# A tenth load for ten DMA engines: 640 columns of w1 on other partitions, and two engines that end in new blocks of instructions

## The chip, the cores and the metric

The kernel runs on one core of a Trainium2 chip. The metric is device microseconds of one execution; the number compared is the median of a few runs. Sixteen DMA engines serve the core, through a queue that SyncE (SP) issues on (q1, hardware) and one that GpSimd (POOL) issues on (q0, software). Instructions arrive by DMA too (q8).

## What is computed

One decode step for two batch rows: attention with grouped heads over the last 4096 positions of a cache, a dense layer with Mish beside it, and a gate that mixes both. All data are float32.

```python
# B=2, D=512, Hq=32, Hkv=8, Dh=128, W=4096, F=1792
x = A_x                                        # [2, 1, 512]
g = sigmoid((x * gate_w).sum(-1, keepdims=True))
q = (x @ wq).reshape(B, 1, Hq, Dh).transpose(0, 2, 1, 3)
k = repeat(k_cache[:, :, Sk - W:, :], 4, axis=1)
v = repeat(v_cache[:, :, Sk - W:, :], 4, axis=1)
p = softmax(einsum("bhqd,bhkd->bhqk", q, k) * Dh ** -0.5)
a = einsum("bhqk,bhkd->bhqd", p, v).transpose(0, 2, 1, 3).reshape(B, 1, Hq * Dh) @ wo
h = x @ w1 + b1                                # Dense -> Mish -> Dense
b = (h * tanh(softplus(h))) @ w2
out = g * a + (1 - g) * b
```

## The kernel before

**Stages.** 91 MB come from HBM once. SyncE issues nearly all loads, each 128 partitions wide, in the order of use: `wq` (8 MB), `small`, then for each of the eight KV heads one load of 8 MB (`kv0` to `kv7`: keys and values of both batch rows), then `w12` (most of w1, and the first rows of wo and w2), the parts of w1 described below, the rest of wo in two loads (5 and 2 MB), and the rest of w2 in three (1024, 512 and 256 KB). Three large buffers (`stream`) rotate, so a load waits until TensorE has finished with the buffer three loads earlier. For each head TensorE computes `scores`, VectorE the maximum, ScalarE the exponential, TensorE turns it (`turned`) and multiplies with the values (`values`). When the last head is done come `hidden` (h = x w1, in `hp`; Mish follows on ScalarE, GpSimd and VectorE), `outputs` (the heads' factors, `ol`), `project` (wo, and the first part of w2, summed in `acc`) and `finish` (the rest of w2, summed in `fin`). A copy and the store end the program. Instructions of each engine run in the order written; `pin` keeps the scheduler from moving one.

**w1 and its moved columns.** w1 has 512 rows, four blocks of 128 (`c` = 0 to 3), and 1792 columns, which `hidden` takes in four groups `j` of 512, 512, 512 and 256. The four groups write to four quarters of `hp`'s partitions. In the last block (c = 3) the 512 columns of group 0 are not part of `w12`. Their 128 rows lie elsewhere: in `ext`, a piece of the buffer of wo, `SLOTS` = 3 rows to a partition, on the partitions that `ROWS_OF` lists (first partition, count, slots). GpSimd clears `ext` with a memset first; the matching values of x stand in `x32[:, 4:7]`, with zeros for all other places. So `hidden` multiplies three slots with `x32` in place of one block. `w12` rows are that much shorter.

**The parts.** Each entry of `ROWS_OF` is one load (`part`). SyncE issues three of them, from five, five and four rows of HBM; GpSimd issues `part2`, eight partitions from two rows of HBM. The number of rows of HBM (`SPLIT`) is the number of DMA engines that share a load. GpSimd issues a tiny load `turn` of seven engines ahead of `part2` and one behind it: 7 + 2 + 7 = 16.

The lines that the prediction's steps touch: the memset of `ext` (L316), `part` (L320), `turn` (L324), the matmuls of `hidden` (L258), `acc` (L348), `fin` (L358), the copy `asum` (L374), and `landed` (L386), where SyncE waits for the last eight loads ahead of the store (L392).

Of the kernel before, what the change touches and what calls it, by code (L numbers as in the profile page):

```python
# [8 lines left out]
F32 = mybir.dt.float32  # L9
# [4 lines left out]
P = 128  # L14
# [12 lines left out]
Q = 32  # L27
RS = Q // B
BH = B * REP
F = 1792  # L30
DC = D // P
FC = F // P
FG = 4
# [1 line left out]
CHUNK = 8192  # L35
HEAD = 2048
SLOTS = 3
APART = ((0, FG),)
WIDTH = sum(n for _, n in APART) * P
ROWS_OF = ((0, 20, 3), (32, 20, 2), (60, 8, 3), (28, 4, 1))  # L40
SPLIT = (5, 5, 2, None)
TURN = 7
GAP = 64
PITCH = 272
W1 = DC * F - WIDTH
# [11 lines left out]
def decode_kernel(ctx: ExitStack, tc: tile.TileContext, res, stored, small, wqh, wqt, kv_in, w12, wo, w2, *rest):  # L57
    *parts, before, behind, out = rest
    nc = tc.nc

    stream = ctx.enter_context(tc.tile_pool(name="stream", bufs=3))
    const = ctx.enter_context(tc.tile_pool(name="const", bufs=1))
# [5 lines left out]
    loads = []  # L68

    def load(name, *parts):  # L70
        t = stream.tile([P, 2 * CHUNK], F32, tag="s", name=name)
        x = 0
        for cols, src in parts:
            loads.append(nc.sync.dma_start(t[:, x : x + cols], src))  # L74
            x += cols
        return t
# [11 lines left out]
                      reason="ScalarE begins behind the first load")  # L88
# [16 lines left out]
    x32 = const.tile([P, DC + SLOTS, Q], F32, name="x32")  # L105
# [51 lines left out]
    pin = tc.keep_in_program_order  # L157

    def scores(kv, t):
        sc = ps_s.tile([P, 512], F32, tag="sc", name=f"sc{kv}")  # L160
        for m in range(BN):
            for j in range(NJ):
                nc.tensor.matmul(sc[Q * j : Q * j + Q, :], qz[:, kv, m * Q : m * Q + Q],  # L163
                                 t[:, (m * NJ + j) * 512 : (m * NJ + j + 1) * 512],
                                 start=(m == 0), stop=(m == BN - 1))
        nc.vector.tensor_reduce(mx[:, kv : kv + 1], sc, axis=AX.X, op=ALU.max, negate=True)  # L166
        p = work.tile([P, 512], F32, tag="p", name=f"p{kv}")
        nc.scalar.activation(p, sc, AF.Exp, bias=mx[:, kv : kv + 1], accum_out=ls[:, kv : kv + 1])  # L168
        return p
# [74 lines left out]
    def hidden(t):  # L244
        hp = ps_s.tile([P, FG * P], F32, tag="sc", name="hp")
        away = dict(APART)
        for c in range(DC + SLOTS):
            for j in range(NJ):
                n = min(FG, FC - j * FG) * P
                if c < DC - 1:  # L250
                    w = t[:, c * F + j * FG * P :]
                elif j in away and c >= DC:
                    w = ext[:, c - DC, P * sum(k for i, k in APART if i < j) :]
                elif j not in away and c == DC - 1:
                    w = t[:, c * F + P * (j * FG - sum(k for i, k in APART if i < j)) :]
                else:
                    continue
                nc.tensor.matmul(hp[Q * j : Q * j + Q, :n], x32[:, c, :], w[:, :n],  # L258
                                 start=(c == 0), stop=(c == (DC + SLOTS if j in away else DC) - 1))
        hs = work.tile([P, FG * P], F32, tag="p", name="hs")  # L260
        nl = (FC - (NJ - 1) * FG) * P
        nc.scalar.copy(hs[:, :nl], hp[:, :nl])
        nc.scalar.copy(hs[: Q * (NJ - 1), nl:], hp[: Q * (NJ - 1), nl:])
        ht = ps_1.tile([P, FG, NJ, Q], F32, tag="pt", name="ht")

        def m(name):
            return const.tile([P, FC, B], F32, name=name)

        h, e, nu, de, ho = (m(x) for x in ("h", "e", "nu", "de", "ho"))
        for k in range(FG):  # L270
            nj = len(range(k, FC, FG))
# [23 lines left out]
    for kv in range(HKV):  # L295
        t = load(f"kv{kv}", (2 * CHUNK, kv_in[kv][:, : 2 * CHUNK]))
        p = scores(kv, t[:, :CHUNK])
# [16 lines left out]
    x = (WO[-1] - WO[0]) * REP * D  # L314
    ext = wo_t[:, x : x + SLOTS * WIDTH].rearrange("p (s w) -> p s w", s=SLOTS)
    nc.gpsimd.memset(ext, 0.0)  # L316

    def part(engine, i):
        p0, n, slots = ROWS_OF[i]
        loads.append(pin(engine.dma_start(ext[p0 : p0 + n, :slots, :].rearrange("p s x -> p (s x)"),  # L320
                                          parts[i][:, : n * slots * WIDTH // parts[i].shape[0]])))

    def turn(name, src):
        pin(nc.gpsimd.dma_start(const.tile([2 * TURN, 2], F32, name=name), src[:, :4]))  # L324

    turn("turn0", before)
    part(nc.gpsimd, 2)
    turn("turn1", behind)
    for i in (0, 1, 3):
        part(nc.sync, i)  # L330
    x = 0
    for cols, src in flat(wo, [f - WO[0] for f in WO], REP * D):
# [2 lines left out]
    x = AHEAD + CUTS[1] * D  # L335
    for cols, src in flat(w2, [f - CUTS[1] for f in CUTS[1:]], D):
        loads.append(nc.sync.dma_start(w12_t[:, x : x + cols], src))
        x += cols
    hidden(w12_t)
    outputs(kf, r)  # L340

    acc = ps_1.tile([P, D], F32, tag="acc", name="acc")
# [25 lines left out]
    for x in range(HQ):  # L368
        w = w12_t[:, W1 + x * D :] if x < first else wo_t[:, (x - first) * D :]
# [1 line left out]
            middle(0, CUTS[1])  # L371
        pin(project(x % REP, oT[:, x, :], w[:, :D], n_of[x % REP]))
    asum = work.tile([P, D], F32, tag="p", name="asum")
    nc.scalar.copy(asum, acc)  # L374

    def output(i):
        for f in range(CUTS[i], CUTS[i + 1]):
# [5 lines left out]
    output(2)  # L383
    output(3)

    landed = nc.sync.nop()  # L386
    for ld in loads[-8:]:
        tc.add_manual_dep(landed.ins, ld.ins.name,
                          mybir.DependencyInfo(mybir.DependencyClass.Sync, mybir.DependencyReason.DATA),
                          reason="SyncE sees the last loads land ahead of the store")  # L390
# [5 lines left out]
                      reason="the store reads the copy")  # L396
# [72 lines left out]
```

## Time and profile before

| | |
|---|---|
| median of 3 runs | 218.88 us (218.82, 218.88, 220.08) |
| the profiled run | 218.95 us |
| its span (first to last instruction) | 217.1 us |
| DMA | 91.38 MB, mean 421 GB/s |
| TensorE busy | 113.3 us (52%) |
| instruction loads (q8) | 6 packets, 0.10 MB |
| GpSimd's queue (q0) | 144 packets, 0.05 MB |

The page of the profile shows busy shares, queues, the chain of work that ended last and the costliest groups of instructions. A group reads: line, engine, operation, tile written <- tiles read. `w` is the tile of `w12`, `wo` holds `ext` as well. The span leaves 218.95 - 217.1 = 1.85 us of the run outside.

### The profile page before, as it was taken

Reading aid. Unit: us, or ns where it says so; the run is one execution under the profiler, and the core shown is the slowest. Engines: PE = TensorE matmul, PEld = TensorE weight load, DVE = VectorE, ACT = ScalarE, POOL = GpSimd, SP = SyncE. Lnnn points to the kernel's source line nnn. Section 1 sums busy time; section 2 is a strip of 40 time slices with the busy share of each in tenths; the row PEclk is TensorE's granted clock in tenths of the full one; section 3 lists DMA queues with packets and bytes.
Section 4 is the critical chain, followed back from the end, with each engine's and each line's share of the span. In section 5 each row is a group of like instructions: output and inputs, shape, how many; then the busy total and the mean of one; then the engine's idle time right before and its main releaser. Section 6 shows DMA issues by size and latency. Waiting matters only on the chain.

```text
span 217.1 us, 1858 instructions
## 1 busy us (share of the span) xinstructions
PE 113.3 (52%) x826; PEld 34.5 (16%) x826; DVE 21.5 (10%) x32; ACT 15.4 (7%) x34; POOL 11.4 (5%) x34
## 2 busy tenths in 40 slices
PE   0000797367055609533770753287066608759995
PEld 0000312112011102101120210012011101213342
DVE  0000000010001320100105010010501001250100
ACT  0200001011002000200010020002002000301001
POOL 8000000000000000000000000000000230100300
PEclk9999999889859975996797699679958957999699
DMA  9798998999989998999999999999999999999894
GB/s 362 338 507 351 546 411 386 399 522 423 399 386 519 426 411 386 495 447 399 399 483 450 399 411 447 483 399 411 450 471 399 423 447 430 430 383 468 377 410 159
DMA packets 2752, 91.38 MB, mean 421 GB/s; under 512 B 566, under 2 KB 646, under 8 KB 954
## 3 DMA queue, kind: packets, MB, share of 16 engines
q1 hardware_dynamic: 2602, 91.24, 97.6%
q8 instruction: 6, 0.10, 0.2%
q0 software_dynamic: 144, 0.05, 0.1%
HBM read 91.24 MB, written 0.04 MB: 421 GB/s over the span
## 4 chain that ended last, share of the span: by engine, by line
DMA 78%; PE 15%; ACT 2%; SPq 2%; DVE 1%; issue 1%; POOL 1%; ACTq 0%
DMA kv<-in_kv 61%; DMA w<-in_w 17%; PE sc L163 8%; PE o L187 5%; ACT p L168 1%; PE fin L358 1%; DVE mx L166 1%; SPq L320 1%; PE pp L175 1%; ACT pT L176 1%; POOL wo L316 1%; SPq L333 0%; SPq L74 0%; SPq L80 0%; DVE res L391 0%
## 5 line engine op out<-in xcount | busy, mean ns | idle before, releaser
L163 PE MATMUL sc<-kv,qz 128*32 128x512 f32 x256 | 43.3, 839 | 54.7 <-DMA kv<-in_kv 54.7
L187 PE MATMUL o<-kv,pT 128*32 128x512 f32 x256 | 29.5, 596 | 5.8 <-ACT pT L176 5.8
L163 PEld LDWEIGHTS sc<-kv,qz 128*32 128x32 f32 x256 | 9.7, 149 | 87.7 <-DMA kv<-in_kv 61.3
L143 PE MATMUL qp<-wq,x 128*32 128x512 f32 x64 | 11.4, 760 | 23.1 <-POOL x L107 23.1
L166 DVE TENSOR_REDUCE mx<-sc 128x1 f32<-128x512 f32 x8 | 5.5, 692 | 112.3 <-PE sc L163 112.3
L168 ACT ACTIVATE p<-sc,mx 128x512 f32<-128x512 f32 x8 | 5.5, 687 | 131.2 <-DVE mx L166 131.2
L175 PE MATMUL pp<-ident,p 128*128 128x128 f32 x32 | 5.2, 286 | 12.1 <-ACT p L168 12.1
L187 PEld LDWEIGHTS o<-kv,pT 128*32 128x32 f32 x256 | 7.3, 109 | 20.9 <-issue 13.2
L316 POOL MEMSET wo<- 128x1536 f32 x1 | 1.4, 1377 | 144.4 <-PE o L187 144.4
L197 DVE TENSOR_REDUCE od<-om 128x256 f32<-128x1024 f32 x4 | 7.6, 1898 | 0.1
L143 PEld LDWEIGHTS qp<-wq,x 128*32 128x32 f32 x64 | 2.4, 134 | 28.7 <-POOL x L107 23.1
L348 PE MATMUL acc<-wo,padded 128*32 128x512 f32 x56 | 6.9, 593 | 0.0
L194 DVE TENSOR_TENSOR om<-o,pick 128x1024 f32<-128x1024 f32 x4 | 4.9, 1225 | 19.3 <-PE o L187 19.3
L175 PEld LDWEIGHTS pp<-ident,p 128*128 128x128 f32 x32 | 3.4, 140 | 18.6 <-ACT p L168 18.6
L176 ACT COPY pT<-pp 128x512 f32<-128x512 f32 x8 | 4.7, 585 | 6.2 <-PE pp L175 6.2
L258 PE MATMUL hp<-w,x 128*32 128x512 f32 (+1 forms) x30 | 3.6, 540 | 2.5 <-DMA w<-in_w 2.5
L348 PE MATMUL acc<-w,padded 128*32 128x512 f32 x22 | 4.3, 896 | 0.4 <-DVE padded L241 0.4
L348 PEld LDWEIGHTS acc<-wo,padded 128*32 128x32 f32 x56 | 2.5, 109 | 3.5 <-issue 2.5
L258 PE MATMUL hp<-wo,x 128*32 128x512 f32 x6 | 2.7, 592 | 0.0
L132 DVE RECIPROCAL g<-g 128x2 f32<-128x2 f32 x1 | 0.2, 165 | 22.4 <-POOL g L131 22.4
L358 PE MATMUL fin<-w,padded 128*32 128x128 f32 x56 | 2.1, 277 | 0.4 <-DMA w<-in_w 0.4
L149 PE MATMUL qt<-ident,qs 128*128 128x128 f32 x8 | 1.3, 286 | 1.4 <-ACT qs L146 1.4
(71 smaller groups left out, 35.8 us busy)
## 6 DMA issues: line engine op xcount, KB each, us to landing
wq<-in_wqt SPq DMA_DIRECT2D x1, 7168.0 KB, 21.5
w<-in_w SPq DMA_DIRECT2D x1, 6144.0 KB, 41.3
wo<-in_wo SPq DMA_DIRECT2D x1, 5120.0 KB, 29.6
wo<-in_wo SPq DMA_DIRECT2D x1, 2048.0 KB, 34.1
wq<-in_wqh SPq DMA_DIRECT2D x1, 1024.0 KB, 4.9
w<-in_w SPq DMA_DIRECT2D x1, 1024.0 KB, 36.0
w<-in_w SPq DMA_DIRECT2D x1, 512.0 KB, 35.4
w<-in_w SPq DMA_DIRECT2D x1, 256.0 KB, 21.1
```

The lines of the kernel that those rows point to most:

```text
L143: nc.tensor.matmul(qp[Q * k : Q * k + Q, :], x32[:, c, :], w[:, c, k, :], start=(c == 0), stop=(c == DC - 1))
L163: nc.tensor.matmul(sc[Q * j : Q * j + Q, :], qz[:, kv, m * Q : m * Q + Q], t[:, (m * NJ + j) * 512 : (m * NJ + j + 1) * 512], start=(m == ...
L166: nc.vector.tensor_reduce(mx[:, kv : kv + 1], sc, axis=AX.X, op=ALU.max, negate=True)
L168: nc.scalar.activation(p, sc, AF.Exp, bias=mx[:, kv : kv + 1], accum_out=ls[:, kv : kv + 1])
L175: pin(nc.tensor.transpose(pp[:, c, :], p[:, c * P : (c + 1) * P], ident))
L176: nc.scalar.copy(pT, pp)
L187: pin(nc.tensor.matmul(o[Q * j : Q * j + Q], pT[:, c, Q * j : Q * j + Q], t[:, (c * NJ + j) * 512 : (c * NJ + j + 1) * 512], start=(c == 0 ...
L194: nc.vector.tensor_tensor(ov, pair[0].rearrange("p k (m d) -> p k m d", m=BN), pick[:, None, :, None].to_broadcast([P, 2, BN, DH]), op=ALU ...
L197: nc.vector.tensor_reduce(od[:, kv - 1 : kv + 1], ov.rearrange("p k m d -> p k d m"), axis=AX.X, op=ALU.add)
L258: nc.tensor.matmul(hp[Q * j : Q * j + Q, :n], x32[:, c, :], w[:, :n], start=(c == 0), stop=(c == (DC + SLOTS if j in away else DC) - 1))
L348: return nc.tensor.matmul(acc[Q * j : Q * j + Q, :], lhsT, rhs, start=(n_col[j] == 1), stop=(n_col[j] == n))
L358: nc.tensor.matmul(fin[Q * j : Q * j + Q, :], lhsT[:, y : y + Q], rhs[:, j * P : (j + 1) * P], start=(done[0] == 0), stop=(done[0] == n_fi ...
```

## The change

Three things change together.

1. 640 columns of w1's last block are moved instead of 512 (`APART`): all of group 0 and the first 128 of group 1. Rows of `w12` get 512 bytes shorter, `ext` gets wider (3 x 640 = 1920 columns instead of 1536), and `hidden` takes group 1 in two pieces: 384 columns from `w12` at c = 3, and 128 columns from `ext` at each of the three slots.
2. The 128 rows lie on other partitions (0 to 19, 32 to 48, 60 to 67 and 84 to 95), and the loads are shared differently: `part0` (20 partitions, 3 slots, five groups), `part1` (five partitions, one slot, five groups), `part2` (three partitions, one slot, three groups) from SyncE, and `part3` (eight partitions, 3 slots, two groups) and `part4` (twelve partitions, 3 slots, three groups) from GpSimd. `turn1` shrinks from seven rows to four: 7 + 2 + 4 + 3 = 16. Five, two and three engines carry parts, ten in all.
3. ScalarE, behind its last copy `asum`, and SyncE, behind a new wait for the last load but one (`early`), jump to the start of a new block of 256 instructions.

```diff
-APART = ((0, FG),)
+APART = ((0, FG), (1, 1))
-ROWS_OF = ((0, 20, 3), (32, 20, 2), (60, 8, 3), (28, 4, 1))
-SPLIT = (5, 5, 2, None)
-TURN = 7
+ROWS_OF = ((0, 20, 1, 3, 5), (32, 5, 4, 1, 5), (33, 3, 4, 1, 3), (60, 8, 1, 3, 2), (84, 12, 1, 3, 3))
+TURNS = (7, 4)
...
-                n = min(FG, FC - j * FG) * P
+                n, a = min(FG, FC - j * FG) * P, away.get(j, 0) * P
+                moved = P * sum(k for i, k in APART if i < j)
                 if c < DC - 1:
-                    w = t[:, c * F + j * FG * P :]
-                elif j in away and c >= DC:
-                    w = ext[:, c - DC, P * sum(k for i, k in APART if i < j) :]
-                elif j not in away and c == DC - 1:
-                    w = t[:, c * F + P * (j * FG - sum(k for i, k in APART if i < j)) :]
+                    x0, x1, w = 0, n, t[:, c * F + j * FG * P :]
+                elif c == DC - 1:
+                    x0, x1, w = a, n, t[:, c * F + j * FG * P - moved :]
                 else:
-                    continue
-                nc.tensor.matmul(hp[Q * j : Q * j + Q, :n], x32[:, c, :], w[:, :n],
-                                 start=(c == 0), stop=(c == (DC + SLOTS if j in away else DC) - 1))
+                    x0, x1, w = 0, a, ext[:, c - DC, moved:]
+                if x1 > x0:
+                    nc.tensor.matmul(hp[Q * j : Q * j + Q, x0:x1], x32[:, c, :], w[:, : x1 - x0],
+                                     start=(c == 0), stop=(c == (DC + SLOTS if a else DC) - 1))
...
     def part(engine, i):
-        p0, n, slots = ROWS_OF[i]
-        loads.append(pin(engine.dma_start(ext[p0 : p0 + n, :slots, :].rearrange("p s x -> p (s x)"),
-                                          parts[i][:, : n * slots * WIDTH // parts[i].shape[0]])))
-
-    def turn(name, src):
-        pin(nc.gpsimd.dma_start(const.tile([2 * TURN, 2], F32, name=name), src[:, :4]))
-
-    turn("turn0", before)
-    part(nc.gpsimd, 2)
-    turn("turn1", behind)
-    for i in (0, 1, 3):
+        p0, n, step, slots, groups = ROWS_OF[i]
+        dst = ext[p0 : p0 + (n - 1) * step + 1 : step, :slots, :].rearrange("p s x -> p (s x)")
+        loads.append(pin(engine.dma_start(dst, parts[i][:, : n * slots * WIDTH // groups])))
+
+    def turn(i, src):
+        pin(nc.gpsimd.dma_start(const.tile([2 * TURNS[i], 2], F32, name=f"turn{i}"), src[:, :4]))
+
+    turn(0, before)
+    part(nc.gpsimd, 3)
+    turn(1, behind)
+    part(nc.gpsimd, 4)
+    for i in range(3):
         part(nc.sync, i)
...
-    nc.scalar.copy(asum, acc)
+    pin(nc.scalar.copy(asum, acc))
+    pin(nc.scalar.addr_align(256, max_nops=0))
...
-    landed = nc.sync.nop()
+    early = pin(nc.sync.nop())
+    tc.add_manual_dep(early.ins, loads[-2].ins.name,
...
+    pin(nc.sync.addr_align(256, max_nops=0))
+    landed = pin(nc.sync.nop())
```

GpSimd's queue behind the last head, before the change (operation, tile written <- read, shape; in brackets what is waited for; `in_part2` is `part2` in HBM):

```order
L316 MEMSET wo_570 128x1536 [waits DMAHW3_49,DMAHW6_49,DMAHW1_49,PE_49]
L324 DMA turn0_572<-in_before 14x1x2
L320 DMA wo_570<-in_part2 8x1x1536 [waits Pool_49]
L324 DMA turn1_575<-in_behind 14x1x2
L211 TENSOR_TENSOR ms_522<-ms_522,top_526 8x16x4 [waits DVE_49,Activation_49]
```

The same place on GpSimd now:

```order
L315 MEMSET wo_570 128x1920 [waits DMAHW3_49,DMAHW6_49,DMAHW1_49,PE_49]
L323 DMA turn0_572<-in_before 14x1x2
L320 DMA wo_570<-in_part3 8x1x1920 [waits Pool_49]
L323 DMA turn1_575<-in_behind 8x1x2
L320 DMA wo_570<-in_part4 12x1x1920
L210 TENSOR_TENSOR ms_522<-ms_522,top_526 8x16x4 [waits DVE_49,Activation_49]
```

One load, `part4`, has come to stand last on GpSimd's queue, behind `turn1`.

TensorE in `hidden` before, from the last two matmuls of c = 3 on (`hp` is written; DMASW are GpSimd's loads, DMAHW SyncE's):

```order
L258 MATMUL hp_585<-w12_568,x32_94 32x256
L258 MATMUL hp_585<-wo_570,x32_94 32x512 [waits DMAHW5_49,DMAHW6_49,DMAHW4_49,DMASW1_49]
L258 MATMUL hp_585<-wo_570,x32_94 32x512 x2
L272 MATMUL ht_607<-ident_79,hs_604 128x128 [waits Activation_49]
L272 MATMUL ht_607<-ident_79,hs_604 128x128
```

And now:

```order
L257 MATMUL hp_586<-w12_568,x32_94 32x384
L257 MATMUL hp_586<-w12_568,x32_94 32x512
L257 MATMUL hp_586<-w12_568,x32_94 32x256
L257 MATMUL hp_586<-wo_570,x32_94 32x512 [waits DMAHW5_49,DMAHW4_49,DMAHW6_49,DMASW3_49,DMASW1_49]
L257 MATMUL hp_586<-wo_570,x32_94 32x128
L257 MATMUL hp_586<-wo_570,x32_94 32x512
L257 MATMUL hp_586<-wo_570,x32_94 32x128
```

Three matmuls of 128 columns have come in, and the first matmul on `ext` waits for one more load of GpSimd, DMASW3, which is `part4`.

More of the change, by code (lines that the diff above doesn't have):

```diff
@@ L384, in decode_kernel @@
     output(3)
-    landed = nc.sync.nop()
+    early = pin(nc.sync.nop())
+    tc.add_manual_dep(early.ins, loads[-2].ins.name,
+                      mybir.DependencyInfo(mybir.DependencyClass.Sync, mybir.DependencyReason.DATA),
+                      reason="SyncE goes on to its next block of instructions")
+    pin(nc.sync.addr_align(256, max_nops=0))
+    landed = pin(nc.sync.nop())
     for ld in loads[-8:]:
@@ L409 @@
     xs = np.zeros((SLOTS, P, B), np.float32)
-    places = [(p0 + k, t) for p0, n, slots in ROWS_OF for k in range(n) for t in range(slots)]
+    places = [(p0 + k * step, t) for p0, n, step, slots, _ in ROWS_OF for k in range(n) for t in range(slots)]
     for i, (p, t) in enumerate(places):
@@ L429 @@
     parts, k = {}, 0
-    for i, ((p0, n, slots), groups) in enumerate(zip(ROWS_OF, SPLIT)):
-        block = outer[k : k + n * slots].reshape(n if groups is None else groups, -1)
-        parts[f"part{i}"] = c(np.pad(block, ((0, 0), (0, 0 if groups is None else GAP))))
+    for i, (_, n, _, slots, groups) in enumerate(ROWS_OF):
+        block = outer[k : k + n * slots].reshape(groups, -1)
+        parts[f"part{i}"] = c(np.pad(block, ((0, 0), (0, GAP))))
         k += n * slots
@@ L451 @@
         **parts,
-        **{n: np.zeros((TURN, 4 + GAP), np.float32) for n in ("before", "behind")},
+        **{n: np.zeros((k, 4 + GAP), np.float32) for n, k in zip(("before", "behind"), TURNS)},
     }
```

## The prediction

> **What bounds the kernel now.** I read the page first (busy shares, DMA queues, the chain of work that ended last), then the chain in order of time, then stretches of the tail.
>
> ```profile
> span 217.1 us, 1858 instructions
> PE 113.3 (52%) x826; PEld 34.5 (16%) x826; DVE 21.5 (10%) x32; ACT 15.4 (7%) x34; POOL 11.4 (5%) x34
> ...
> q1 hardware_dynamic: 2602, 91.24, 97.6%
> q8 instruction: 6, 0.10, 0.2%
> q0 software_dynamic: 144, 0.05, 0.1%
> ...
> DMA 78%; PE 15%; ACT 2%; SPq 2%; DVE 1%; issue 1%; POOL 1%; ACTq 0%
> ```
>
> The sixteen DMA engines are busy 97.6% of the span with SyncE's loads, and 78% of the chain is DMA. The kernel is a stream of 91 MB; compute must only keep up. What a change can do is seen at the end:
>
> ```profile
> 176.77 36.03 DMA w<-in_w
> 212.80 0.14 issue
> 212.93 2.26 PE fin L358 x64
> 215.21 0.29 DVE res L391
> ```
>
> Loads set the end until about 214.7, and then come the last matmuls, one copy and the store. TensorE is less idle there than its 52% suggests; these are its groups from the hidden layer on (start, length; in brackets the idle time before, and what ended it):
>
> ```profile
> 193.64 2.77 PE L258 MATMUL hp<-w,x 128*32 128x512 f32 x26 [2.51 <-DMA w<-in_w]
> 196.24 0.59 PE L258 MATMUL hp<-wo,x 128*32 128x512 f32 x1
> ...
> 197.10 1.88 PE L258 MATMUL hp<-wo,x 128*32 128x512 f32 x4
> ...
> 202.23 3.85 PE L348 MATMUL acc<-w,padded 128*32 128x512 f32 x19 [0.43 <-DVE padded L241]
> ...
> 206.04 6.49 PE L348 MATMUL acc<-wo,padded 128*32 128x512 f32 x55
> ...
> 210.40 1.21 PEld L348 LDWEIGHTS acc<-wo,padded 128*32 128x32 f32 x16 [0.50 <-DMA wo<-in_wo]
> ...
> 212.93 1.08 PE L358 MATMUL fin<-w,padded 128*32 128x128 f32 x32 [0.41 <-DMA w<-in_w]
> ...
> 214.72 0.16 PEld L358 LDWEIGHTS fin<-w,padded 128*32 128x32 f32 x8 [0.26 <-DMA w<-in_w]
> ```
>
> After 196.24 TensorE waits for a load only three times: 0.50, 0.41 and 0.26, together 1.17 us. Its other waits there are for ScalarE, VectorE and GpSimd, on work that hangs on the hidden layer and would move with it. So 1.17 us is all the slack: a delay of the hidden layer beyond that comes out at the end, one for one.
>
> **The change part by part.** The part with a price is the new load `part4`, which GpSimd issues last, behind `turn1`. The rows of GpSimd's queue (its issues in time, then KB and us to landing, then packets of each queue in one stretch, 179 to 191 us):
>
> ```profile
> 172.22 1.38 POOL L316 MEMSET wo<- 128x1536 f32 x1 [144.39 <-PE o L187]
> 173.54 0.80 POOL L324 DMA_DIRECT2D turn<-in_before  x1
> 174.33 0.59 POOL L320 DMA_DIRECT2D wo<-in_part  x1
> 174.90 0.57 POOL L324 DMA_DIRECT2D turn<-in_behind  x1
> ...
> wo<-in_part POOLq DMA_DIRECT2D x1, 48.0 KB, 16.5
> ...
> turn<-in_before POOLq DMA_DIRECT2D x1, 0.1 KB, 7.6
> turn<-in_behind POOLq DMA_DIRECT2D x1, 0.1 KB, 18.9
> ...
> q1 hardware_dynamic: 102, 4.92, 94.7%
> q0 software_dynamic: 102, 0.05, 1.4%
> ```
>
> 48 KB need 16.5 us, though all three are issued by 175.5. The counts say why: 102 packets of GpSimd's queue against 102 of SyncE's, one for one. A SyncE packet there has 4.92 MB / 102 = 48 KB, one row of w12, and takes 12 us x 16 / 102 = 1.88 us; every tiny packet of GpSimd waits for one. Of the 144 in the run each engine has nine. They divide as 2 (`turn0`) + 5 (`part2`: four rows and a signal) + 2 (`turn1`): `turn0` lands at 173.54 + 7.6 = 181.1, `part2` at 174.33 + 16.5 = 190.8, and 9.7 us / 1.88 = 5.2 turns; `turn1` lands at 174.90 + 18.9 = 193.8. Nobody waits for `turn1`, and `part2` is needed only at about 196: it has 5 us to spare.
>
> `part4` has four rows to an engine as well, so five more turns behind `turn1`, fourteen in all. By then w12 is through and the packets between are those of `wo`, in the stretch 195 to 203 us:
>
> ```profile
> q1 hardware_dynamic: 83, 3.40, 98.2%
> ```
>
> That is 8 x 16 / 83 = 1.54 us a packet. Five turns are 7.7 us. From 191, where some engines reach `turn1`, this gives a landing at 198.7; from its last landing, 193.8, it gives 201.5. The engines that carry the rows pay for 30.7 KB besides, 1.1 us at 421 / 16 = 26.3 GB/s, and the slowest engine decides. I take 200.5.
>
> TensorE's first matmul on `ext` now waits for this load, and its queue runs in order: behind it stand the six matmuls on `ext`, the transposes `ht`, `ol` and all of `acc`, and ScalarE, VectorE and GpSimd wait for those. It starts at 200.55 instead of 196.24: **+4.3 us**. The three waits for loads go, since loads are not delayed by TensorE here (no later load needs a buffer): **-1.17 us**. At the end +3.15 us.
>
> The clock may add to that or take away:
>
> ```profile
> 202.20:205.60 3.40, 3.37 (x20) 0.85 (x23) 0.27 (x1) 0.00 (x0) 0.64 (x3) 0.54 0.82 352
> ```
>
> In this stretch the granted clock is 0.54, behind the thin work of `ht` and `ol`; it costs 0.46 x 3.4 = 1.6 us today. A pause of four us may move it, drop it or add another: -1.6 to +1.6, and I take nothing. The Trainium skill ("TensorE: Matmul & The Clock Gate", section "HAM oscillation — how this bites in real kernels") warns of TensorE idle gaps over some 3.4 us, after which the clock is halved; the row agrees that a thin stretch is followed by half speed, and by that rule the sum would be 1.6 us more.
>
> The other edits:
> - **Bytes.** Every engine carries 4 KB less of w12 (8 rows, 512 B each). The five engines of `part0` carried 40 to 42 KB of parts and now 32.5 to 35: with w12, 11.3 to 13.8 KB less, -0.43 to -0.52 us. The two of `part3` get 2 KB more, +0.08; three engines that had no part get 26.6 KB more, +1.01; the other six lose 4 KB, -0.16. The tail shows what that can bring (the last columns: granted clock, DMA share, GB/s):
>
> ```profile
> 213.00:213.20 0.20, 0.20 (x12) 0.20 (x16) 0.00 (x0) 0.19 (x1) 0.00 (x0) 1.00 0.79 317
> 213.20:213.40 0.20, 0.20 (x17) 0.20 (x9) 0.00 (x0) 0.00 (x0) 0.00 (x0) 1.00 0.78 307
> 213.40:213.60 0.20, 0.20 (x17) 0.20 (x12) 0.00 (x0) 0.00 (x0) 0.00 (x0) 1.00 0.73 287
> 213.60:213.80 0.20, 0.20 (x16) 0.20 (x11) 0.00 (x0) 0.00 (x0) 0.00 (x0) 1.00 0.67 256
> 213.80:214.00 0.20, 0.20 (x16) 0.16 (x8) 0.00 (x0) 0.00 (x0) 0.00 (x0) 1.00 0.51 195
> 214.00:214.20 0.20, 0.20 (x14) 0.11 (x8) 0.00 (x0) 0.00 (x0) 0.00 (x0) 1.00 0.25 92
> 214.20:214.40 0.20, 0.20 (x15) 0.20 (x14) 0.00 (x0) 0.00 (x0) 0.00 (x0) 1.00 0.06 21
> ```
>
> At 213.0 about three engines (0.21 x 16) are through, and the last at 214.35. Work left at 213.0 is 0.2 x the sum of the shares, 0.76 us if spread evenly: a perfect balance ends loads at 213.76, 0.6 us sooner. If the early three are those that get 26.6 KB, they end at 214.0 and the last of the others 0.16 to 0.5 sooner: 0.25 us gained. All of it lies under TensorE's delay in my forecast and counts for nothing.
> - **The memset** of `ext` grows from 1536 to 1920 columns, 1.38 x 1.25: +0.34 us, and GpSimd issues one more DMA (0.59). Nothing on GpSimd follows until the kernel's last softmax, ten us later; SyncE's parts, released by the memset, queue behind w12's rows (8 x 1.88 us) anyway. Without that cover 0.34.
> - **Three matmuls more** of 128 columns (two passes each). On their own they would take a quarter of the 0.43 us at which the `hp<-wo` matmuls follow each other, 0.64 in all; matmuls on another quarter of the columns run beside them (196.24 and the `hp<-w` rows around it), so I take 0.
> - **Blocks of 256.** The 826 matmuls and 826 weight loads are 6.5 blocks, and q8 loaded six, 0.10 / 6 MB = 16 KB each. ScalarE and SyncE entering a new block should each cause one more, around 213 to 217. One takes
>
> ```profile
> q8 instruction: 1, 0.02, 5.0%
> ```
>
> 5.0% of sixteen engines over 1.2 us (209.9 to 211.1), 0.96 us of one engine. Late loads no longer set the end in my forecast, so it costs nothing unless it meets the store (below). The span leaves 218.95 - 217.1 = 1.85 us of the profiled run outside; that a block loaded early shortens this is possible, and I count 0, the most being 1.85.
>
> **Sum:** 218.95 + 4.3 - 1.17 = 222.1 us for a run like the profiled one, which stands 0.07 above the median of 218.88. Predicted: 222.1.
>
> **The rivals.**
> 1. **Part4 comes in time: not slower.** If the engines served several of GpSimd's packets in one turn once w12 is through, `part4` would land right behind `turn1`, 193.8 + 1.1 = 194.9, before TensorE asks at 195.8. The point from which it decides is a landing after about 197.4 (196.24 + 1.17). Then the balance shows: 218.95 - 0.25 = 218.7. Against it: one for one over all 102 packets, with no exception in twelve us. For it: the stretch with `wo` rows between has no software packet to show. The Trainium skill ("DMA: Bandwidth & Descriptors", section "Queues, rings and completion order") says that an engine drains a whole packet, typically 9 to 17 descriptors, before it turns to the next queue. By that rule the five would go at once and the time would be this rival's; the trace disagrees as far as it goes.
> 2. **The change doesn't hit the light engines.** If the three engines that get `part4` are not the early ones but carry instruction loads, the last of them ends at 214.35 + 1.01 = 215.4: with rival 1's timely landing 218.95 + 1.0 = 219.95. Under my forecast TensorE covers it.
> 3. **The new blocks collide.** An instruction load of 0.96 us on an engine that still has rows, or that carries a piece of the store, delays the end by up to 0.96: 219.9 with rival 1, 223.1 with the forecast. If SyncE had to wait for its block ahead of the store, the price is the load after the wait for the last rows but one, again about one us.
>
> **How the numbers follow.** Forecast 0.77, by itself 220.0 to 224.2: the early landing (-1.8), the late one (+1.0), the clock (1.6 either way, not all at once), the small matmuls (+0.64) and a collision (+0.96). Rival 1 alone 0.12, with 2 or 3 on top 0.05 (218.3 to 220.0). A landing so late, or a second slow stretch, that it passes 224.2: 0.04; faster by shortening what lies outside the span, 0.02. Range 220.0 to 224.2. A measurement of this kernel tells about 1% from no change: 216.7 to 221.1. Of the forecast 0.69 lies above and 0.08 within. So slower 0.73, within 1% 0.26, faster 0.01.
>
> **What would show it.** A wait of TensorE for the load from `in_part` at the first `hp<-wo` matmul, some 4 to 5 us long; software packets still running at 195 to 200 us, 224 of them in all (14 x 16); no wait for loads at `acc` and `fin`; 8 instruction loads instead of 6; DMA idle in the last 4 us of compute. If the wait is missing and the time is near 218.7, the turns were wrong; if the wait is there and the end moves less, my slack of 1.17 or the clock was.

## The result and the profile after

| | before | after |
|---|---|---|
| median | 219.04 us (218.82 to 220.08, 4 runs) | 223.95 us (223.35 to 225.58, 4 runs) |
| the profiled run, its span | 218.95, 217.1 us | 223.52, 221.6 us |

The change makes the kernel slower: ratio 1.024, 95% interval 1.0208 to 1.0272. The forecast was 222.1, in a range of 220.0 to 224.2. So the direction and the place were right, and the loss is 4.9 us where 3.2 were forecast.

TensorE in the profile after, from the hidden layer on (start, length; in brackets the idle time before, and what ended it; `issue` means that the view doesn't name who ended it):

```profile
193.50 3.63 PE L257 MATMUL hp<-w,x 128*32 128x512 f32 x30 [1.06 <-DMA w<-in_w]
201.69 4.08 PE L257 MATMUL hp<-wo,x 128*32 128x512 f32 x12 [4.56 <-issue]
206.25 0.65 PE L271 MATMUL ht<-ident,hs 128*128 128x128 f32 x4 [0.48 <-ACT hs L261]
...
209.04 2.41 PE L348 MATMUL acc<-w,padded 128*32 128x512 f32 x19 [0.42 <-DVE padded L240]
...
211.31 6.14 PE L348 MATMUL acc<-wo,padded 128*32 128x512 f32 x52
...
218.84 0.84 PE L358 MATMUL fin<-w,padded 128*32 128x128 f32 x24
```

The first matmul on the moved columns waits 4.56 us and starts at 201.69; it was 196.24. No wait for a load is left at `acc` and `fin`. The loads of the same run (GpSimd's issue of `part4`; queues with packets, MB and share; then KB and us from issue to landing; then packets of both queues from 179 to 191 us, and of GpSimd's from 195 to 203):

```profile
175.41 0.60 POOL L320 DMA_DIRECT2D wo<-in_part  x1
...
q0 software_dynamic: 224, 0.15, 0.2%
q8 instruction: 6, 0.10, 0.2%
q14 instruction: 4, 0.03, 0.0%
...
wo<-in_part POOLq DMA_DIRECT2D x1, 90.0 KB, 26.2
...
q1 hardware_dynamic: 108, 4.96, 95.4%
q0 software_dynamic: 108, 0.06, 1.7%
...
q0 software_dynamic: 34, 0.05, 1.6%
```

108 packets against 108, 224 in all, and 34 still after 195: GpSimd's packets again go one for one with SyncE's. It holds behind w12 too, where the trace of the kernel before had no packet of GpSimd to show: in the packet records each of `part4`'s twelve rows is followed by a packet of SyncE, eleven times a row of `wo` (40 KB, 1.51 us). `part4` lands at 175.41 + 26.2 = 201.6, and TensorE starts 0.1 later. Two stretches of TensorE's clock (third column from the end):

```profile
201.00:204.40 3.40, 2.71 (x10) 1.11 (x11) 0.00 (x0) 0.00 (x0) 0.00 (x0) 0.50 0.95 410
209.00:212.40 3.40, 3.36 (x32) 0.99 (x35) 0.28 (x1) 0.00 (x0) 0.64 (x3) 1.00 0.97 401
```

The half-speed stretch that lay in `acc` before (0.54 from 202.2 to 205.6) now lies right behind the pause, in `hp`, and `acc` has the full clock.

**The account.** The last group of `fin` in the kernel before:

```profile
214.09 1.06 PE L358 MATMUL fin<-w,padded 128*32 128x128 f32 x24
```

From the first matmul on the moved columns to the last of `fin`, before took 215.15 - 196.24 = 18.91 us (214.09 + 1.06), after 219.68 - 201.69 = 17.99 (218.84 + 0.84). So the start costs 5.45 and the rest gives 0.92 back: +4.53, against 4.57 between the two profiled runs. Within the 0.92: `hp` +1.34 (4.08 for 2.74), `acc` and `fin` together 10.64 for 12.92, which is 2.28 less. The first row of `acc` alone is 1.44 shorter (2.41 for 3.85), which I put down to the clock. That leaves 0.84 for the waits for loads, where 1.17 were priced; the split is a subtraction, not a measurement.

### The profile page after: what moved, and what is told of

It is laid out like the page before. It is cut to its first block, busy times and chain, and to the rows that moved or that the text cites. A ratio compares the mean times of both kernels' runs of the same rounds, so it can differ in the third digit from the quotient of the medians.

```text
span 221.6 us, 1874 instructions
## 1 busy us (share of the span) xinstructions
PE 117.7 (53%) x832; PEld 35.3 (16%) x832; DVE 21.6 (10%) x32; ACT 15.5 (7%) x34; POOL 12.3 (6%) x35
## 4 chain that ended last, share of the span: by engine, by line
DMA 59%; PE 24%; another core or an unknown queue 11%; ACT 3%; DVE 2%; issue 1%; SPq 1%; POOL 0%; ACTq 0%; DVEq 0%; POOLq 0%
DMA kv<-in_kv 59%; PE sc L162 11%; PE o L186 6%; PE acc L348 4%; ACT p L167 1%; DVE mx L165 1%; PE pp L174 1%; PE fin L358 1%; ACT pT L175 1%; PE ol L238 1%; SPq L73 0%; PE ht L271 0%; POOL ms L210 0%; SPq L79 0%
## 5 line engine op out<-in xcount | busy, mean ns | idle before, releaser
L162 PE MATMUL sc<-kv,qz 128*32 128x512 f32 x256 | 46.2, 888 | 52.3 <-DMA kv<-in_kv 52.3
L186 PE MATMUL o<-kv,pT 128*32 128x512 f32 x256 | 31.0, 621 | 5.8 <-ACT pT L175 5.8
L315 POOL MEMSET wo<- 128x1920 f32 x1 | 1.7, 1697 | 144.1 <-PE o L186 144.1
L257 PE MATMUL hp<-wo,x 128*32 128x512 f32 (+1 forms) x12 | 4.1, 629 | 4.6 <-issue 4.6
L257 PE MATMUL hp<-w,x 128*32 128x512 f32 (+2 forms) x30 | 3.6, 533 | 1.1 <-DMA w<-in_w 1.1
L348 PE MATMUL acc<-w,padded 128*32 128x512 f32 x22 | 2.8, 601 | 0.4 <-DVE padded L240 0.4
L257 PEld LDWEIGHTS hp<-wo,x 128*32 128x32 f32 x12 | 1.2, 153 | 7.4 <-issue 7.3
```

What stands on the lines that cost most here:

```text
L186: pin(nc.tensor.matmul(o[Q * j : Q * j + Q], pT[:, c, Q * j : Q * j + Q], t[:, (c * NJ + j) * 512 : (c * NJ + j + 1) * 512], start=(c == 0 ...
L257: nc.tensor.matmul(hp[Q * j : Q * j + Q, x0:x1], x32[:, c, :], w[:, : x1 - x0], start=(c == 0), stop=(c == (DC + SLOTS if a else DC) - 1))
L348: return nc.tensor.matmul(acc[Q * j : Q * j + Q, :], lhsT, rhs, start=(n_col[j] == 1), stop=(n_col[j] == n))
```

## The experiments

The theory is that `part4`'s late turns cost the time, through TensorE's wait; the rivals are the new blocks, the moved bytes, the three small matmuls and the clock. Ratios below are to the kernel before, whose median was 218.79 to 218.87 us beside these runs.

**1. The parts without the blocks, and the blocks without the parts.** `parts_only`:

```diff
-    pin(nc.scalar.addr_align(256, max_nops=0))
...
-    pin(nc.sync.addr_align(256, max_nops=0))
```

> The changed kernel without the two jumps to new blocks (ScalarE's and SyncE's), all loads and matmuls as changed. Theory of the turns (part4 needs five turns of GpSimd's queue behind turn1, TensorE waits for it): part4 lands at 201 to 202 us, TensorE waits as long as with the jumps, and the time stays at 223 to 225 us, within 0.5% of the changed kernel. Theory of the blocks (the jumps cost at the end): at least 1 us faster than the changed kernel's 223.95.

Measured: 225.01 us (1.0302, 1.0238 to 1.0365), so all of the loss and a little more. The landing and two rows of TensorE:

```profile
200.59 4.38 PE L257 MATMUL hp<-wo,x 128*32 128x512 f32 x12 [3.17 <-issue]
...
208.24 4.04 PE L348 MATMUL acc<-w,padded 128*32 128x512 f32 x19 [0.43 <-DVE padded L240]
...
wo<-in_part POOLq DMA_DIRECT2D x1, 90.0 KB, 25.0
```

It starts 1.1 us sooner than the changed kernel and still ends later, since here both `hp` (4.38) and `acc` (4.04 for 2.41) are slow: two stretches at half clock (below). `blocks_only` puts the jumps, and the wait `early` ahead of SyncE's, into the kernel before:

```diff
+    pin(nc.scalar.addr_align(256, max_nops=0))
...
+    pin(nc.sync.addr_align(256, max_nops=0))
```

> The kernel before with the two jumps to new blocks alone. In the changed kernel SyncE spent 2.5 us in its jump (branch at 214.93, next instruction at 217.44), under cover of TensorE's delay. Here there is no cover: the jump would begin at 214.0, when the last load but one lands, and end at 216.5, and the store would be issued at 216.6 instead of 215.53: 1.1 us slower, 220.0 us. If a new block shortens what lies outside the span, or the block is there already, the time stays at 218.9 or falls.

Measured: 220.22 us (1.0068, 1.0051 to 1.0085). The last copy and the store (SyncE):

```profile
215.19 0.29 DVE L397 COPY res<-fin 128x128 f32<-128x128 f32 x1 [12.88 <-PE fin L358]
...
216.80 0.35 SPq L398 DMA_DIRECT2D out<-res  x1
```

The store is issued 1.61 us behind the copy. In the kernel before it came 0.32 behind (the copy starts at 215.21):

```profile
215.53 0.35 SPq L392 DMA_DIRECT2D out<-res  x1
```

In the changed kernel it is 0.32 too: there TensorE ends 4.5 us later, and SyncE, through with its jump, waits 2.4 us for the copy. So the jumps cost 1.36 us by themselves and are covered in the changed kernel. They don't explain the loss.

**2. The same load through SyncE.** `part4_sync`, without the jumps too:

```diff
-TURNS = (7, 4)
+TURNS = (7, 7)
...
-    part(nc.gpsimd, 4)
-    for i in range(3):
+    for i in (0, 1, 2, 4):
         part(nc.sync, i)
```

> The changed kernel without the jumps, with part4 issued by SyncE instead of GpSimd (then on the first three engines, which carry part0 too), and turn1 of seven rows. Theory of the turns: the wait of TensorE is gone, hp<-wo begins at about 196 as before the change; the three engines carry 19.5 KB more than in the kernel before, 0.73 us, so the last load lands at 215.4 and the time is 219.7 us. If the slowdown comes from the bytes moved or from the matmuls, it stays at 222 us or more.

Measured: 220.54 us (1.0077, 1.0062 to 1.0092). The wait is gone, and waits for loads are back:

```profile
195.90 0.59 PE L257 MATMUL hp<-wo,x 128*32 128x512 f32 x1
...
207.05 4.50 PE L347 MATMUL acc<-wo,padded 128*32 128x512 f32 x40 [0.67 <-DMA wo<-in_wo]
211.90 1.92 PE L347 MATMUL acc<-wo,padded 128*32 128x512 f32 x16 [0.35 <-DMA wo<-in_wo]
214.42 1.08 PE L357 MATMUL fin<-w,padded 128*32 128x128 f32 x32 [0.60 <-DMA w<-in_w]
```

Same bytes, same partitions, same small matmuls, and 4.5 us less than `parts_only`. So they are not the main cost. That 1.7 us remain was not expected in this size: `fin` starts 1.5 us later than before, on loads.

**3. Turns without bytes.** `before_late` and `before_late2` put three and two tiny loads ahead of `part2` in the kernel before, six and four turns more:

```diff
     turn("turn0", before)
+    tiny = const.tile([16, 12], F32, name="tiny")
+    for i in range(3):
+        pin(nc.gpsimd.dma_start(tiny[:, 4 * i : 4 * i + 4], small[:16, :4]))
     part(nc.gpsimd, 2)
```

> The kernel before with three more tiny loads (16 rows of 16 bytes) on GpSimd ahead of part2: six more turns on each engine, no byte of w1 moved. Theory of the turns: 15 x 16 = 240 packets in q0, part2 lands at about 200 us instead of 190.8, TensorE's first hp<-wo matmul starts then instead of at 196.24, and the time is 221.5 to 223.5 us. If the turns don't matter, 219.0 us.

> The kernel before with two tiny loads of 16 rows ahead of part2 on GpSimd's queue, four turns more (three tiny loads, six turns, moved its landing from 190.8 to 198.5 and gave 222.84 us). No byte of w1 is moved. Theory of turns, with 1.88 us a turn while w12 runs and 1.54 behind it: 11 turns for part2, 190.8 + 4 x 1.8 = 197 to 198 us; TensorE asks at 195.8, so it waits 1.2 to 2.2 us, of which 1.17 us are won back at the loads for which it then need not wait: 218.9 to 220.0 us if the clock behaves as before. If a wait of this length already drops the clock: 220.0 to 221.5. Software packets 208 in all. Rival (the number of packets ahead does not matter, only bytes): 218.9 us with part2 at 191.

Measured: 222.84 us with three (1.0133, 1.006 to 1.0207; one of the four runs took 219.74), 218.89 with two (1.000, 0.9991 to 1.0008). `part2` and TensorE, with three:

```profile
wo<-in_part POOLq DMA_DIRECT2D x1, 48.0 KB, 24.2
...
199.25 4.39 PE L258 MATMUL hp<-wo,x 128*32 128x512 f32 x6 [2.09 <-DMA wo<-in_part]
```

and with two (issued at 174.46):

```profile
wo<-in_part POOLq DMA_DIRECT2D x1, 48.0 KB, 21.9
...
196.38 0.62 PE L258 MATMUL hp<-wo,x 128*32 128x512 f32 x1
```

In three of its four runs, less than one KB in tiny packets makes the kernel before 4 us slower: the place in the queue is enough. Why the fourth took 219.74 is open; it has no profile. With seven turns `part2` lands at 190.8, with eleven at 196.4, with thirteen at 175.01 + 24.2 = 199.2: 1.4 us for each turn, on average. With eleven it lands when TensorE asks, and costs nothing. My 197 to 198 for eleven was 1 us late.

**4. Fewer turns for the changed kernel.** In `merged` and `merged_mid` one load of five engines takes the place of `part3` and `part4`, and a tiny load goes to the start of the kernel (jumps out in both; `merged` has one tiny load of 11 rows and none behind):

```diff
-ROWS_OF = ((0, 20, 1, 3, 5), (32, 5, 4, 1, 5), (33, 3, 4, 1, 3), (60, 8, 1, 3, 2), (84, 12, 1, 3, 3))
+ROWS_OF = ((0, 20, 1, 3, 5), (32, 5, 4, 1, 5), (33, 3, 4, 1, 3), (60, 20, 1, 3, 5))
...
+    pin(nc.gpsimd.dma_start(const.tile([2 * TURNS[0], 2], F32, name="turn0"), before[:, :4]))
     queries(0, wq_t[:, :CHUNK])
```

> The changed kernel without both jumps to new blocks, and with the rows of part3 and part4 in one load of GpSimd (20 partitions, five engines); one tiny load of 11 rows ahead of it, issued long before w12 is asked for; nothing behind it. GpSimd's packets: 2 + 5 turns as far as the load that TensorE needs, as in the kernel before, instead of 14. Theory of turns: the load lands by 188 to 191, TensorE does not wait for it, the first matmul on the moved columns starts at 195.8 to 196.3. Then only the bytes are left of the change: 218.6 if the engines with the new bytes had time to spare, 219.0 to 219.7 if two of them also carry instruction loads and end the loads at 215.3. Rival (the moved bytes, or the three partial matmuls, cost the 5 us): 222.5 to 224.

> As the merged load, but the sixteen engines are taken in another order: a tiny load of 7 rows early, the merged load on the next five engines, and a tiny load of 4 rows behind it, for which nobody waits. The five engines with the bytes of the late loads are others than in the merged kernel. Theory of turns: no wait for the load either, first matmul on the moved columns at 195.8 to 196.3. Theory of engines (the engines that carry instruction loads end last; two of the three engines of part4 did): the end of the loads moves against the merged kernel by up to 1 us, 218.3 to 219.7 in all, and the lower of the two times belongs to the kernel whose five engines carry fewer instruction loads. Rival (the share of the engines does not matter): the same time as the merged kernel within 0.2 us.

Measured: `merged` 221.63 us (1.0125, 1.0109 to 1.0141), `merged_mid` 219.75 (1.0047, 1.003 to 1.0065). `merged_mid` at the first matmul on the moved columns and at `fin`:

```profile
195.99 0.59 PE L257 MATMUL hp<-wo,x 128*32 128x512 f32 x1
...
213.58 1.08 PE L357 MATMUL fin<-w,padded 128*32 128x128 f32 x32 [0.60 <-DMA w<-in_w]
```

No wait for the part, 4.2 us less than the changed kernel, and 0.9 more than before: that is what is left of the change without its wait. `fin` starts 0.65 later than before, on loads. `merged` has no wait for its part either (it lands by 190). It waits for `w12` itself; its row, and the stretch 179 to 191 us of `merged` and then of `merged_mid` (last columns: DMA share, GB/s):

```profile
195.79 4.47 PE L257 MATMUL hp<-w,x 128*32 128x512 f32 x26 [3.68 <-DMA w<-in_w]
...
179.00:191.00 12.00, 9.72 (x64) 2.77 (x68) 2.15 (x6) 1.81 (x5) 0.67 (x3) 0.84 0.98 374
```

```profile
179.00:191.00 12.00, 9.92 (x72) 2.80 (x64) 2.16 (x6) 1.81 (x5) 0.89 (x3) 0.86 0.97 420
```

In `merged` the engines are as busy and move 11% less. In its packet records a row of `w12` takes up to 2.31 us between 180 and 188 (the median is 2.22), where it takes 1.80 in `merged_mid`. Why is open; neither of the two theories spoke of it, and with it in between the two times don't test the theory of engines.

**5. `part4` ahead of `turn1`.** `swap`, without the jumps; `swap_early` also issues `turn0` at the start of the kernel:

```diff
-    turn(1, behind)
     part(nc.gpsimd, 4)
+    turn(1, behind)
```

> The changed kernel without both jumps (225.01 us), with one line moved: GpSimd issues part4 ahead of turn1. Same bytes, same rows, same 224 packets; only part4 no longer stands behind turn1's two turns (12 in place of 14), and its engines are 9 to 11 of the row in place of 13 to 15. Theory of turns: from the measured landings, 11 turns gave no wait (218.89) and 13 a wait of 2.1 us (222.84), so 12 turns land at 197.5 to 199, TensorE waits 1 to 2.5 us, and the run takes 219.7 to 222.5, according to whether one or two stretches at half clock follow. Rival (five turns of part4 itself behind part3 are what counts, not its place): 225.

> As the kernel with part4 ahead of turn1, and turn0 issued at the start of the kernel, before the queries, as in the merged_mid kernel: ten turns ahead of and with part4. Theory of turns: lands at about 195, TensorE asks at 195.8, no wait; the moved bytes lie on the same five engines as in merged_mid (219.75 us), so 219.4 to 220.2. Rival (two loads of GpSimd are dear by themselves, however placed): 222 or more.

Measured: 221.63 us (1.0113, 1.0084 to 1.0143) and 220.7 (1.0099, 1.007 to 1.0128). TensorE in `swap`, its row of `part4`, and packets of the stretch 188 to 196 us in `swap`, then in the changed kernel:

```profile
194.68 5.33 PE L257 MATMUL hp<-w,x 128*32 128x512 f32 x30 [3.47 <-DMA w<-in_w]
201.25 2.73 PE L257 MATMUL hp<-wo,x 128*32 128x512 f32 x12 [1.24 <-issue]
...
wo<-in_part POOLq DMA_DIRECT2D x1, 90.0 KB, 25.8
...
q1 hardware_dynamic: 116, 2.76, 90.0%
q0 software_dynamic: 94, 0.10, 4.2%
```

```profile
q1 hardware_dynamic: 128, 3.25, 94.6%
q0 software_dynamic: 103, 0.07, 2.7%
```

Here my theory missed. The time lies where I expected it, but not for the reason: twelve turns should have landed `part4` by 199, and it starts TensorE at 201.25, no sooner than fourteen do. The stretch has the slow rows of `merged`: SyncE's queue moves 2.76 MB where it moves 3.25 in the changed kernel, in 116 turns for 128, and GpSimd's turns are late with them. `swap_early`, with ten turns, starts at 197.86 where about 195 was expected, with slow rows too:

```profile
197.86 2.74 PE L257 MATMUL hp<-wo,x 128*32 128x512 f32 x12 [0.18 <-issue]
```

So counting turns is not enough where the rows between them get slow. Both gained on the changed kernel; `swap` because it has no stretch at half clock behind the start.

**6. The clock.** `warm` runs 36 matmuls in the pause, into a PSUM tile that nobody reads; `warm2` runs 20 there and 4 each behind `hidden`, `ht` and `ol`:

```diff
+            for i in range(36 if c == DC else 0):
+                pin(nc.tensor.matmul(dm[Q * (i % NJ) : Q * (i % NJ) + Q, :], x32[:, 0, :], t[:, :512],
+                                     start=True, stop=True))
```

and `warm2`, where `warm(n)` is these n matmuls:

```diff
+            warm(20 if c == DC else 0)
...
+        warm(4)
         ht = ps_1.tile([P, FG, NJ, Q], F32, tag="pt", name="ht")
...
     hidden(w12_t)
+    warm(4)
     outputs(kf, r)
+    warm(4)
```

> The changed kernel with 36 matmuls more in front of the first matmul on the moved columns, on w12's data and into a PSUM tile that nobody reads. They need nothing from the late load, so TensorE runs them in the pause in which it waits for part4. Theory (the pause of 4.6 us costs the clock, and the clock costs 1.34 us in the matmuls behind it): the load still lands at about 201.5 and TensorE still cannot start on it before, but the granted clock stays whole, the twelve records of hp<-wo take 2.7 us instead of 4.08, and the run takes 1.3 us less than the changed kernel, 222.0 to 223.0, ratio to before about 1.017. If acc and fin lose the full clock in exchange (another half-speed stretch later, as in the kernel before), it is 223.0 to 224.5. Rival (the twelve records are slow because they wait for the load's last rows, not for the clock): their 4 us stay and the run takes 223.5 to 224.3, like the changed kernel.

> The changed kernel with 20 matmuls in the pause (not 36, which ran 1.9 us past the landing of part4) and 4 each behind hidden's last matmul, behind the four transposes ht and behind ol, all into a PSUM tile that nobody reads. Theory (each tail has one stretch of 3.4 us at half clock behind its thinnest place, and it costs 1.3 to 1.6 us wherever it falls): if the 20 carry the clock over the pause and the twelve over ht and ol, there is no stretch left, first matmul on the moved columns at 201.7, then 2.75 us for it and 8.7 for acc: 222.2 to 222.9. If the stretch still comes in acc, the run takes what the changed kernel takes, 223.7 to 224.5, and the clock was even between before and after. Rival (the clock plays no part): 224.0 plus up to 1 us for the added matmuls.

Measured: 225.49 us (1.0299, 1.0284 to 1.0314) and 224.75 (1.0266, 1.0212 to 1.032; 223.0 to 226.12). Stretches of `warm`, one right behind the pause and one in `acc`:

```profile
203.40:206.20 2.80, 2.80 (x20) 1.11 (x12) 0.00 (x0) 0.00 (x0) 0.00 (x0) 1.00 0.79 334
209.60:213.00 3.40, 3.40 (x20) 0.78 (x20) 0.11 (x1) 0.00 (x0) 0.64 (x3) 0.50 0.95 396
```

Stretches of `swap`, one while TensorE still multiplies the columns from `w12`, ahead of its wait, and one behind the start on the moved columns; then both half-speed stretches of `parts_only`:

```profile
195.20:198.60 3.40, 3.40 (x25) 0.86 (x19) 0.00 (x0) 0.00 (x0) 0.00 (x0) 0.51 0.99 412
201.20:204.60 3.40, 2.87 (x13) 1.00 (x14) 0.00 (x0) 0.56 (x2) 0.00 (x0) 1.00 0.90 388
```

```profile
201.50:204.90 3.40, 3.40 (x7) 0.44 (x5) 0.00 (x0) 0.00 (x0) 0.00 (x0) 0.51 0.81 349
...
208.40:211.80 3.40, 3.40 (x20) 0.79 (x17) 0.08 (x1) 0.00 (x0) 0.64 (x3) 0.50 0.96 405
```

In `warm` the pause no longer costs the clock, but the stretch comes back in `acc`. Its 36 matmuls hold TensorE for 1.8 us past the landing at 201.6, and its median is 1.5 above the changed kernel's. `warm2` has the whole clock from 200.6 to 217.0 in its profiled run, and that run takes 223.0, only 0.5 less than the changed kernel's, though its `part4` lands 1 us sooner: from the start to the last of `fin` it takes 18.37 us, 1.7 more than `swap` without the twelve matmuls.

```profile
200.60:217.00 16.40, 16.40 (x139) 6.64 (x139) 0.84 (x4) 0.86 (x3) 1.99 (x8) 1.00 0.76 319
```

As a way to win the 1.3 us back both failed. What they show is that stretches can be moved and avoided, and from the other kernels follows what one costs. The last groups of `fin` in `swap`, `parts_only` and the second profile of the changed kernel (experiment 7):

```profile
217.06 0.84 PE L358 MATMUL fin<-w,padded 128*32 128x128 f32 x24
...
219.68 0.84 PE L358 MATMUL fin<-w,padded 128*32 128x128 f32 x24
...
218.20 0.84 PE L358 MATMUL fin<-w,padded 128*32 128x128 f32 x24
```

From the first matmul on the moved columns to the last of `fin` it takes:

| stretches at half clock behind the start | kernel | us |
|---|---|---|
| none | `swap` | 16.65 |
| one | changed kernel, its two profiles | 17.99, 18.29 |
| two | `parts_only`, `before_late` | 19.93, 19.93 |

So the first costs 1.3 to 1.6 us, and two cost 3.3.

**7. The changed kernel once more.**

> The changed kernel as it is, once more, for a second profile and more times. Theory: its time is the start of the first matmul on the moved columns, plus a length from there to the last matmul of fin that goes by the number of stretches at half clock (16.6 us with none, 18.0 with one, 19.9 with two, as measured in the swap kernel, the changed kernel and the kernel without jumps). The start hangs on the slowest of part4's three engines: 200.2 to 200.7 if none of them had an instruction load earlier, 201.3 to 201.8 if one had (such an engine runs 1.4 us late). So the runs fall between 221.5 and 226, the median within 0.5% of the first 223.95, and the profiled run is met by the sum of its two terms plus 4.0 us (start of the run's clock, last copy and store) within 0.3 us. Rival (the time is spread by something else): a profile whose start and length don't give its time.

Measured: 224.34 us (1.0266, 1.0207 to 1.0324; 223.03 to 225.78), the profiled run 223.60.

```profile
200.75 4.39 PE L257 MATMUL hp<-wo,x 128*32 128x512 f32 x12 [4.04 <-issue]
...
wo<-in_part POOLq DMA_DIRECT2D x1, 90.0 KB, 25.5
...
out<-res SPq DMA_DIRECT2D x1, 40.0 KB, 2.3
```

`part4` lands 0.9 us sooner than in the first profile, at 175.18 + 25.5 = 200.7. From the start to the last of `fin` it takes 18.29, with one stretch. The sum, 200.75 + 18.29 + 4.0 = 223.04, misses the run by 0.56, more than the 0.3 I allowed. The last row tells where: the store takes 2.3 us instead of 1.5. It took 2.2 in `warm`, and 1.5 in the other three profiles with the jumps. One of the new blocks' instruction loads lies in the time of the store in this profile and in `warm`, but one does so in the first profile too; that it met an engine which carries a piece of the store is a guess that no run tests.

What makes the landing differ is seen by following the engines through the packet records (they don't name the engine; a packet is given to the one whose last packet ended where it starts). The first profile, for the three engines that carry `part4`, us:

```
last row of kv7 ends | GpSimd's first packet | first and last row of part4 | part4's last packet
177.0                | 178.8                 | 192.9  198.3                | 200.1
178.1                | 179.9                 | 194.1  199.4                | 201.2
178.3                | 178.3                 | 192.7  196.6                | 198.4
```

Two of the three are late at the end of `kv7`, and so are two others of the sixteen; four loads of 16 KB of instructions had come by then (46.34, 77.75, 113.93, 152.77). But being late isn't what decides. One of the two took two of GpSimd's packets ahead of its first row of `w12` and was through first. The other was free a little sooner, took that row first, and its fourteenth turn came last of all: this sets the landing. In `parts_only` two of the three engines are late as well, both took GpSimd's packets first and were through at 198.2, and the landing (200.5) is that of the third. In the second profile of the changed kernel none of the three is late: their rows of `part4` begin between 192.8 and 193.0, and their last packets come at 200.0 to 200.2. So the bounds that I gave above for an engine with an instruction load don't hold.

## Why the prediction was right or wrong

- **Turns: right in kind and in size.** One for one, 224 packets, and `part4` late. From `turn1`'s last packet to `part4`'s the engine that is last takes 201.24 - 192.54 = 8.70 us (five rows of `wo` at 1.51 and four of its own at 0.29), where I had 7.7 + 1.1. (30.7 KB at 26.3 GB/s are 1.17, not 1.1.)
- **The step that failed: the landing of `part4`, and with it TensorE's start, +5.45 instead of +4.3.** I took 200.5, which is 8.8 behind 191.7, and gave no reason for this place between my bounds of 198.7 and 201.5. The engine that came last was through with `turn1` only at 192.54, and `part4` landed at 201.6, just past the later bound. TensorE starts 0.1 behind it. So this term is 1.15 of the 1.4 us by which the account of the profiled runs exceeds the sum. Three other profiles with fourteen turns land at 200.5, 200.6 and 200.7, and `warm` at 201.6 again: my value was one of two that occur, by luck, and one value for all executions was too few.
- **In the second profile of the changed kernel other terms are off.** There the start is only 0.2 later than forecast (200.75). The time from there to the last of `fin` gives back 0.62 instead of 1.17, and the store takes 0.8 more, which the sum had at nothing.
- **The three waits: gone, as forecast, and worth less.** By the subtraction above they gave 0.84 of 1.17 us. Two of the three (0.50 and 0.26) were idle time of weight loads, which run beside the matmuls.
- **The clock: no net change in the profiled run, as taken, but by luck.** One stretch before, one after, moved from `acc` to `hp` (-1.44 and +1.34). Profiles of kernels near it have none or two. Executions of the changed kernel run from 223.0 to 225.8, while the kernel before stays within 0.5 in most, and the median of the changed kernel stands 0.4 above its profiled run. The landing and the number of stretches could make this spread; both profiles of the changed kernel have one stretch, so this is not shown. The Trainium skill ("TensorE: Matmul & The Clock Gate", section "HAM oscillation — how this bites in real kernels") says that idle gaps over some 3.4 us halve the clock. Behind the gap of 4.56 the trace agrees. By that rule alone the sum would have been 1.6 us more; the runs show that the stretch in `acc` went in exchange. In `before_late` half speed came behind an idle time of 2.09 too, so here the length of the gap alone doesn't tell.
- **Bytes: no gain seen, and hidden.** I took 0.25 us as a gain. The kernels where TensorE doesn't wait for the part are slower than before: 0.9 us in `merged_mid`, 1.7 in `part4_sync`, with `fin` later on loads in both. This is the second rival's direction; that an engine with new bytes ends last there is likely, not shown, and both share the bytes otherwise than the changed kernel. In the changed kernel TensorE's delay covers it.
- **Blocks: covered, with another price and another queue.** Six loads in q8 as before, and four of 8 KB in q14, where I had eight in q8. Alone they cost 1.36 us, through SyncE's store, near the one us of the third rival. A store 0.7 to 0.8 us longer, which may be its collision, came in two of the five profiles with the jumps.
- **The small matmuls, memset and issue: nothing seen**, as taken. `merged_mid`, with all of them, starts the moved columns at 195.99.
- **The first rival** (several packets in one turn, 218.7 us) is out: 108 against 108, a packet of SyncE behind each row of `part4`, and the 4 us of `before_late` for packets almost without bytes. The rule that stands behind it, in the Trainium skill ("DMA: Bandwidth & Descriptors", section "Queues, rings and completion order"), has an engine drain a packet of typically 9 to 17 descriptors in a turn. The trace disagrees: behind each of `part4`'s rows stands a packet of SyncE.

No version with the moved columns beat the kernel before; the nearest, `merged_mid`, is 0.5% slower.

## What to carry to other kernels

A load that GpSimd issues beside a full SyncE queue is priced more by its packets than by its bytes: count how many of GpSimd's packets stand ahead of its last one on an engine, multiply by the time of a SyncE row, and compare with the time at which the data is needed. In the kernel before, four more turns were free and six cost 4 us. The count can fall short: `swap` and `swap_early` landed some 2 to 3 us behind it. And the slowest of the engines that carry the load decides, so allow for more than one landing. Where a late load stops TensorE, look at the clock behind the stop as well, and at more than one execution, since a stretch at half speed may move, vanish or double.

## What the runs showed of the hardware that I had not expected

- An instruction load of 16 KB makes one DMA engine late by about 1.4 us: in the first profile of the changed kernel the one at 192.37 took 0.89 us, and the row behind it 2.06 instead of 1.51. In every profile four of the sixteen engines end `kv7` about 1.4 us behind the others, as many as such loads had come by then. Which row such an engine takes first when GpSimd's packets arrive can move the landing of a load on few engines by 1 us.
- A jump to a new block near the end held the store back by 1.3 us, though SyncE jumped before its last wait for loads.
- Most of SyncE's rows became slower for some us in `merged` (2.22 us for 1.80, median from 180 to 188), `swap` and `swap_early` (1.77 and 1.73 for 1.51, from 188 to 196), and not in `merged_mid` or the changed kernel. What sets this off stays open.
